# Pooled attention with a feed-forward behind it: the first weights' conversion put at other steps of a pair

## The chip, the cores and the metric

The kernel runs on one core of a Trainium2 chip. The metric is the device time of one execution in microseconds. A change is judged against the kernel before, timed on the same chip.

## The reference

Attention over 4 x 8 heads of 1152 keys and a head size of 64. Two neighbouring queries are averaged, so 576 are left; the scores are scaled, the row maximum is taken off, and the exponentials are normalised. The result, 2304 tokens of 512, goes through a feed-forward layer with 2048 hidden units:

```python
q_pool = q.reshape(B, H, S // 2, 2, D).mean(axis=3)
scores = scale * np.matmul(q_pool, k.transpose(0, 1, 3, 2))
attn = np.exp(scores - np.max(scores, axis=-1, keepdims=True))
attn = attn / (np.sum(attn, axis=-1, keepdims=True) + 1e-09)
x = np.matmul(attn, v)            # then heads side by side: (2304, 512)
r = np.maximum(x @ w_in, 0.0)
out = (s * (r * r) + b) @ w_out
```

The two weight matrices arrive as 64-bit floats. The kernel turns each into two 32-bit parts, hi and lo.

## The kernel before, in words

The kernel has two stages. The attention runs over 32 heads, two heads (a pair) at a time, 16 pairs from 0 to 15; the feed-forward layer follows.

A head has 9 steps, one for each block of 128 keys, so a pair has 18 steps, and a step number below is n % 18 of the loop over n. In a step TensorE makes the scores of one block (`score_step`, tile s, L486), ScalarE takes their exponentials (L490, L495, L498), and, where the step's kind in `KIND` asks for a high and a low part, VectorE (kind v) or GpSimd (kind g) makes pl, what the rounded exponential ph leaves over (L501). Kind w makes neither. The kinds of a pair are vwvgvwvgw, twice. GpSimd's pl belong to steps 3, 7, 12 and 16. Three steps later (`LAG`) TensorE multiplies the exponentials by v (`value_step`, tile o): L518 for kind w, else L524, L526 (with vl, the low part of v) and L528 (with pl). The order of TensorE's products in a step is written out in `ORD`.

Fifteen steps ahead, `max_unit` makes the scores again at lower cost (tile m, L456) and VectorE takes their row maximum (tile pm, L457) for the shift of a later head. Tile m has two PSUM banks, so a product waits until VectorE is through with the maximum two before it; tile s has two banks as well. At steps 2 and 11 `finish` copies the sums of a head out (ScalarE), and after the odd head VectorE inverts them (`XT`: transposes lt and rr, a reciprocal), and GpSimd scales (xo).

Other work of a pair stands at fixed steps: `PREP` prepares the pair after the next (transposes on VectorE at steps 10 to 12; on GpSimd qs at 9, kh at 11 and 12, kl at 12, qh and qz at 13, ql at 14); `prep_v` splits the next head's v at steps 7 and 16 (GpSimd, vv then vl); `load_k` and `load_q` follow at 14, `load_v` at 3 and 12, and `lay`, the copies of k and q into their tiles, at 4 and 13. All these DMAs are issued by SP, in that order; ScalarE issues the two small ones of the shift.

Engines work through their own queues in the order in which the program emits. What is put off goes through `later(k, fn)`, and `tick()` runs at the end of each step what is due. Put off by 0 or 1, an operation comes at the end of the same step; put off by k, ahead of the work of k steps on. Operations due at the same tick run by due time, then in the order in which they were put off.

The weights of the first three blocks of 128 hidden units are converted inside the attention (`conversions`, called with `wstage`, `STA` and no PSUM pool): six chunks of 128 x 512, w_in and w_out by turns. `CB` and `CP` say at which n a call comes: seven calls, 18 steps apart, the last at n = 274, step 4 of pair 15. A call at chunk i fetches chunk i + 1 (one DMA of 512 KB on SP) and starts `narrow(i)`, which has these parts, put off by the numbers of `STA`:

- s0 (L151, L153): ScalarE takes the absolute value of the high words into hm and scales the low words into R
- s1 (L159), s1b (L163), s1c (L166): VectorE clamps hm, shifts its bits and joins them with the sign into A
- s2 (L169, L170): VectorE keeps the exponent of A (ab), ScalarE rounds A to hi
- s3 (L174), s4 (L177), s5 (L180): GpSimd multiplies R by ab, subtracts hi from A, and adds both into lo

The tiles hm, ab, A and R exist once each, the raw chunk twice. Before the change s0 comes at the end of step 4, s1, s1b and s1c all ahead of step 8, s2 ahead of step 10, and s3, s4 and s5 ahead of steps 13, 15 and 17. Pairs 10 to 15 convert one chunk each; pair 9 has the first fetch alone. The other 26 chunks are converted in the feed-forward stage with other numbers (`STB`) and a PSUM tile.

```python
    def tick():
        step[0] += 1
        due = sorted(x for x in queue if x[0] <= step[0])
        queue[:] = [x for x in queue if x[0] > step[0]]
        for _, _, fn in due:
            fn()
...
            if (CB - n) % CP == 0 and 0 <= CB - n < 7 * CP:
                weights_a()
        tick()
```

Of the kernel before, what the change touches and what calls it, by code (L numbers as in the profile page):

```python
# [12 lines left out]
AF = mybir.ActivationFunctionType  # L13
# [27 lines left out]
VS = (7, 16)  # L41
XT = (1, 2, 3, 4, 8)
SW = (3, 9)
CB, CP = 274, 18
WB = (7, 11)
STA = (0, 4, 4, 4, 6, 9, 11, 13)
STB = (0, 1, 2, 3, 4, 5, 6, 8)
MO = (2, 3, 6)
XS = (1, 2)
# [3 lines left out]
def f32(ap):  # L53
    return ap.bitcast(F32)
# [3 lines left out]
def attention_moe_kernel(ctx: ExitStack, tc: tile.TileContext, q, k, v, w_in, w_out, s_in, b_in, out):  # L58
    nc = tc.nc
# [35 lines left out]
    def weight_tiles(pool, f0, f1):  # L95
        n = f1 - f0
        ih = pool.tile([P, NC, n * P], F32R, name=f"wih{f0}")
        il = pool.tile([P, NC, n * P], F32R, name=f"wil{f0}")
        oh = pool.tile([P, n, DM], F32R, name=f"woh{f0}")
        ol = pool.tile([P, n, DM], F32R, name=f"wol{f0}")  # L100
        for i in range(n):
            f = f0 + i
            wi_hi[f] = ih[:, :, i * P:(i + 1) * P]
            wi_lo[f] = il[:, :, i * P:(i + 1) * P]
            wo_hi[f] = oh[:, i, :]
            wo_lo[f] = ol[:, i, :]

    def conversions(pool, stage, f0, f1, bufs, stages, psum=None):

        weight_tiles(pool, f0, f1)
        chunks = []
        for f in range(f0, f1):
            chunks.append((w_in[:, f * P:(f + 1) * P].rearrange("(c p) f -> p c f", p=P), wi_hi[f], wi_lo[f], f"i{f}"))
            chunks.append((w_out[f * P:(f + 1) * P, :].rearrange("p (c f) -> p c f", c=NC),
                           wo_hi[f].rearrange("p (c f) -> p c f", c=NC), wo_lo[f].rearrange("p (c f) -> p c f", c=NC), f"o{f}"))
        wide = w_in.dtype == mybir.dt.int64
        raw = {}  # L120
        state = [-1]

        def done(i):
            f = f0 + i // 2
            ready[f] = ready.get(f, 0) + 1

        def tmp(tag, name):
            return stage.tile([P, NC, P], F32, tag=tag, bufs=bufs, name=f"{tag}{name}")

        def fetch(i):  # L130
            src, _, _, name = chunks[i]
            if wide:
                raw[i] = stage.tile([P, NC, 2 * P], I32, tag="wst", bufs=2, name=f"wst{name}")
                nc.sync.dma_start(raw[i], src.bitcast(I32))
            else:
                raw[i] = stage.tile([P, NC, P], F32, tag="wst", bufs=2, name=f"wst{name}")
                nc.sync.dma_start(raw[i], src)

        def narrow(i):
            _, hi, lo, name = chunks[i]  # L140
            words = raw.pop(i).rearrange("p c (n w) -> p c n w", w=2)
            high, low = words[:, :, :, 1].bitcast(F32), words[:, :, :, 0].bitcast(U32)
            hm, ab, A, R = (tmp(t, name) for t in ("whm", "wab", "wA", "wR")) if psum is None else (None, *(tmp(t, name) for t in ("wab", "wA", "wR")))

            bank = None if psum is None else psum.tile([P, 512], F32, tag="w", bufs=1, name=f"w{name}").rearrange("p (c f) -> p c f", c=NC)
            hm, bits, full = (hm, ab, A) if psum is None else (bank, bank, bank)
            hmi, biti, abi, fulli, top = (t.bitcast(I32) for t in (hm, bits, ab, full, high))
            eng = nc.gpsimd if psum is None else nc.vector

            def s0():  # L150
                nc.scalar.activation(hm, high, AF.Abs)  # L151
                if psum is None:
                    nc.scalar.activation(R, low, AF.Copy, scale=2.0 ** -52)  # L153
                else:
                    nc.gpsimd.tensor_scalar(out=R, in0=low, scalar1=2.0 ** -52, scalar2=0.0, op0=ALU.mult, op1=ALU.add)

            def s1():

                nc.vector.tensor_scalar(out=hm, in0=hm, scalar1=W_MIN, scalar2=W_MAX, op0=ALU.max, op1=ALU.min)  # L159

            def s1b():

                nc.vector.tensor_scalar(out=biti, in0=hmi, scalar1=0x07FFFFFF, scalar2=3, op0=ALU.bitwise_and, op1=ALU.logical_shift_left)  # L163

            def s1c():
                nc.vector.scalar_tensor_tensor(out=fulli, in0=top, scalar=-0x40000000, in1=biti, op0=ALU.bitwise_and, op1=ALU.bitwise_or)  # L166

            def s2():
                nc.vector.tensor_scalar(out=abi, in0=fulli, scalar1=-0x800000, scalar2=None, op0=ALU.bitwise_and)  # L169
                nc.scalar.activation(hi, full, AF.Copy)  # L170

            def s3():

                nc.gpsimd.tensor_tensor(out=R, in0=R, in1=ab, op=ALU.mult)  # L174

            def s4():
                eng.tensor_tensor(out=A, in0=full, in1=f32(hi), op=ALU.subtract)  # L177

            def s5():
                nc.gpsimd.tensor_tensor(out=lo, in0=A, in1=R, op=ALU.add)  # L180
                done(i)

            for at, fn in zip(stages, (s0, s1, s1b, s1c, s2, s3, s4, s5)):
                later(at, fn)

        def split(i):
            _, hi, lo, _ = chunks[i]
            st = raw.pop(i)
            nc.scalar.activation(hi, st, AF.Copy)

            def rest():
                nc.gpsimd.tensor_tensor(out=lo, in0=st, in1=f32(hi), op=ALU.subtract)
                done(i)

            later(stages[4], rest)

        def go():
            i = state[0]
            if i >= len(chunks):
                return False  # L200
            if i + 1 < len(chunks):
                fetch(i + 1)
            if i >= 0:
                (narrow if wide else split)(i)
            state[0] += 1
            return True

        return go
# [12 lines left out]
    def later(k, fn):  # L221
        step[1] += 1
        queue.append((step[0] + k, step[1], fn))
# [393 lines left out]
    lays = {}  # L617
    weights_a = conversions(wa, wstage, 0, SW[0], 1, STA)
    NS = NH * NJ
# [132 lines left out]
```

## Time and profile before

| what | us |
|---|---|
| three runs | 971.0, 973.78, 974.75; median 973.78 |
| the profiled execution, its own time | 976.95 |
| its span, first to last instruction | 975.2 |
| mean granted TensorE clock in it | 0.997 of full speed |
| busy: TensorE, VectorE, ScalarE, GpSimd | 922.3, 627.0, 545.9, 507.5 |

The profile is of one execution. Times in it count from the first instruction. Each engine has a timeline; an instruction's row gives its start, its duration, its line in the kernel, the tiles it writes and reads, their shapes, and in square brackets how long the engine stood idle before it and what ended that. The chain of waits follows the end of the program back to what released each step. The granted clock is what the chip allowed TensorE, as a share of 2.4 GHz. The attention's last score product starts at 553.2 us of the span, the first product of the feed-forward layer at 557.2.

### The profile page before, as it was taken

What the parts mean: (1) busy time and instruction counts of PE and PEld (TensorE: products, weight loads), DVE (VectorE), ACT (ScalarE), POOL (GpSimd) and SP (SyncE); (2) the same over time, 40 slices, a digit from 0 to 9 for tenths busy, and PEclk for the clock granted to TensorE, in tenths of its full rate; (3) what the DMA queues carried; (4) which work ended last, traced back from release to release, by engine and by line L of the source; (5) the groups of instructions that cost most, each with busy time, mean ns of one, the idle gap of its engine ahead of it and who ended that gap; (6) DMA issues with size and microseconds to landing.
All of it is one profiled execution on the core that took longest, in us unless ns stands there. A gap on an engine that the chain in (4) does not pass through costs nothing.

```text
span 975.2 us, 16173 instructions
## 1 busy us (share of the span) xinstructions
PE 922.3 (95%) x5712; PEld 821.4 (84%) x5712; DVE 627.0 (64%) x1168; ACT 545.9 (56%) x1054; POOL 507.5 (52%) x405
## 2 busy tenths in 40 slices
PE   4999999999999998988989989999999999999998
PEld 3888888888888887877877877889999899999997
DVE  5777776777677776876875376776776653334333
ACT  2766666666676675665767755554444443333332
POOL 6567656665667568568665567665353430110000
PEclk9999999999999999999999999999999999999999
DMA  8878776777767776676754155663544332222211
GB/s 149 167 145 169 158 152 122 154 168 147 134 138 167 156 152 147 153 142 138 165 146 102 35 162 164 205 217 130 174 130 158 104 136 78 66 87 90 84 44 44
DMA packets 255312, 131.17 MB, mean 135 GB/s; under 512 B 203776, under 2 KB 227328, under 8 KB 255232
## 3 DMA queue, kind: packets, MB, share of 16 engines
q1 hardware_dynamic: 244512, 129.62, 55.0%
q10 hardware_dynamic: 10720, 0.52, 0.7%
q8 instruction: 46, 0.75, 0.3%
q14 instruction: 34, 0.28, 0.1%
HBM read 68.68 MB, written 18.87 MB: 90 GB/s over the span
## 4 chain that ended last, share of the span: by engine, by line
PE 67%; ACT 12%; POOL 7%; DVE 5%; DMA 3%; issue 3%; ACTq 1%; SPq 0%; DVEq 0%; POOLq 0%
PE h L272 18%; PE y L299 17%; PE s L486 12%; PE o L518 5%; PE m L456 5%; PE o L524 4%; PE o L528 4%; PE o L526 4%; ACT ph L495 3%; ACT xu L544 2%; ACT l L545 2%; ACT s L498 2%; POOL pl L501 1%; DVE pm L457 1%; DMA wsto<-in_moe_w_out_dram 1%
## 5 line engine op out<-in xcount | busy, mean ns | idle before, releaser
L457 DVE TENSOR_REDUCE pm<-m 128x1 f32<-128x384 f32 x432 | 230.6, 549 | 112.8 <-PE m L456 106.9
L486 PE MATMUL s<-qq,kk 128*128 128x288 f32 x1152 | 217.6, 311 | 10.9 <-ACT pe L498 7.8
L272 PE MATMUL h<-x,wih 128*128 128x256 f32 x1152 | 213.3, 283 | 7.1 <-DVE gl L286 6.0
L272 PEld LDWEIGHTS h<-x,wih 128*128 128x128 f32 x1152 | 186.0, 189 | 22.1 <-DVE gl L286 6.4
L495 ACT ACTIVATE ph<-s 128x576 fp32r<-128x576 f32 x192 | 125.2, 652 | 132.4 <-PE s L486 109.8
L486 PEld LDWEIGHTS s<-qq,kk 128*128 128x128 f32 x1152 | 175.6, 191 | 27.2 <-ACT pe L498 11.0
L501 POOL TENSOR_TENSOR pl<-pe,ph 128x576 fp32r<-128x576 f32 x64 | 91.5, 1429 | 141.8 <-ACT pe L498 131.2
L272 PE MATMUL h<-x,wil 128*128 128x256 f32 x576 | 162.2, 282 | 0.0
L456 PE MATMUL m<-kh,qz 128*128 128x384 f32 x384 | 156.9, 418 | 3.2 <-DVE pm L457 3.1
L253 POOL TENSOR_TENSOR x<-xr,x 128x1024 fp32r<-128x1024 f32 x27 | 65.0, 2406 | 152.0 <-ACT x L212 143.1
L280 DVE SCALAR_TENSOR_TENSOR h<-h,sb,r 128x256 f32<-128x256 f32 x144 | 70.2, 487 | 114.5 <-ACT r L289 114.5
L524 PE MATMUL o<-ph,vv 128*128 128x288 f32 x384 | 119.0, 310 | 7.8 <-issue 4.8
L518 PE MATMUL o<-pe,vf 128*128 128x288 f32 x384 | 126.0, 412 | 0.0
L528 PE MATMUL o<-pl,vv 128*128 128x288 f32 x384 | 113.6, 296 | 7.3 <-POOL pl L501 7.3
L289 ACT ACTIVATE r<-h 128x256 f32<-128x256 f32 x144 | 55.6, 386 | 110.0 <-PE h L272 109.8
L501 DVE TENSOR_TENSOR pl<-s,ph 128x576 fp32r<-128x576 f32 x128 | 96.2, 752 | 30.9 <-ACT s L498 24.7
L526 PE MATMUL o<-ph,vl 128*64 128x288 f32 x384 | 113.6, 296 | 0.0
L299 PE MATMUL y<-wol,gh 128*128 128x512 f32 x288 | 113.1, 393 | 0.0
L299 PE MATMUL y<-woh,gl 128*128 128x512 f32 x288 | 112.9, 392 | 0.0
L299 PE MATMUL y<-woh,gh 128*128 128x512 f32 x288 | 112.6, 391 | 0.0
L272 PEld LDWEIGHTS h<-x,wil 128*128 128x128 f32 x576 | 109.6, 190 | 0.0
L283 ACT ACTIVATE gh<-h,sb 128x256 fp32r<-128x256 f32 x144 | 68.0, 473 | 64.6 <-DVE h L280 64.3
(89 smaller groups left out, 1508.6 us busy)
## 6 DMA issues: line engine op xcount, KB each, us to landing
kk<-kh SPq DMA_DIRECT2D x32, 576.0 KB, 6.0
kraw<-in_k_dram SPq DMA_DIRECT2D x64, 144.0 KB, 3.5
vf<-in_v_dram SPq DMA_DIRECT2D x32, 288.0 KB, 4.0
kk<-kT SPq DMA_DIRECT2D x32, 288.0 KB, 4.6
qq<-qh SPq DMA_DIRECT2D x64, 144.0 KB, 5.8
xr<-xd SPq DMA_DIRECT2D x18, 512.0 KB, 4.1
qraw<-in_q_dram SPq DMA_DIRECT2D x122, 72.0 KB, 2.5
wsti<-in_moe_w_in_dram SPq DMA_DIRECT2D x16, 512.0 KB, 4.9
```

Source lines behind the costliest of these rows:

```text
L272: nc.tensor.matmul(h[:, :TB], st[:, c, :], mv[:, c, :], start=(n == 0), stop=(n == 3 * NC - 1))
L280: nc.vector.scalar_tensor_tensor(out=t, in0=h[:, :TB], scalar=sb[:, 0:1], in1=r, op0=ALU.mult, op1=ALU.mult)
L299: nc.tensor.matmul(y[:, :DM], st[:, ts_], mv, start=(first and n == 0), stop=(last and n == 2))
L456: nc.tensor.matmul(ps[:, :KB], st, khs[p][:, e * KB:(e + 1) * KB], start=True, stop=True)
L457: nc.vector.tensor_reduce(out=pms[p][:, col, e:e + 1], in_=ps[:, :KB], axis=AX.X, op=ALU.max)
L486: nc.tensor.matmul(ps[:, a, :HALF], kk[:, i, j * P:(j + 1) * P], qq[:, i, a], start=(i == 0), stop=(i == 1))
L495: nc.scalar.activation(ph, ps[:, :, :HALF], AF.Exp, scale=SCALE)
L501: fresh.append(lambda: eng.tensor_tensor(out=pl, in0=full, in1=f32(ph), op=ALU.subtract))
L518: nc.tensor.matmul(o[:, :HALF], vfs[hd % 2][:, j], ph[:, a], start=first, stop=last)
L524: nc.tensor.matmul(o[:, :HALF], vv[:, j], ph[:, a], start=first, stop=False)
L526: nc.tensor.matmul(o[0:D, :HALF], vl[:, j], ph[:, a], start=False, stop=False)
L528: nc.tensor.matmul(o[:, :HALF], vv[:, j], pl[:, a], start=False, stop=last)
```

## The change

The calls come four steps earlier, at step 0 of a pair (`CB` 270 instead of 274), so the fetch of the next chunk does too. `STA` has new numbers: s0 at the end of step 0 with s1 right behind it, s1b ahead of step 3, s1c ahead of step 5, s2 ahead of step 7, and s3, s4, s5 ahead of steps 0, 1 and 2 of the next pair. R, the scaled low words, is made in s2 instead of s0 for these chunks. (Its one tile is still read by s5 of the chunk before until step 2.) The feed-forward stage's conversions stay as they are.

```diff
-CB, CP = 274, 18
+CB, CP = 270, 18
 WB = (7, 11)
-STA = (0, 4, 4, 4, 6, 9, 11, 13)
+STA = (0, 1, 3, 5, 7, 18, 19, 20)
...
             def s0():
                 nc.scalar.activation(hm, high, AF.Abs)
-                if psum is None:
-                    nc.scalar.activation(R, low, AF.Copy, scale=2.0 ** -52)
-                else:
+                if psum is not None:
                     nc.gpsimd.tensor_scalar(out=R, in0=low, scalar1=2.0 ** -52, scalar2=0.0, op0=ALU.mult, op1=ALU.add)
...
             def s2():
                 nc.vector.tensor_scalar(out=abi, in0=fulli, scalar1=-0x800000, scalar2=None, op0=ALU.bitwise_and)
                 nc.scalar.activation(hi, full, AF.Copy)
+                if psum is None:
+                    nc.scalar.activation(R, low, AF.Copy, scale=2.0 ** -52)
```

## Rows read from the trace of the kernel before

Rows of a timeline: start us, duration us, engine, line, operation, tiles, shapes, count, [idle us before it <- what ended it].

**Rows 1.** The page's chain that ended last, share of the span by engine

```profile
PE 67%; ACT 12%; POOL 7%; DVE 5%; DMA 3%; issue 3%; ACTq 1%; SPq 0%; DVEq 0%; POOLq 0%
```

**Rows 2.** TensorE's timeline: first score product of pairs 9, 10 and 14 (start, us)

```profile
315.23 0.91 PE L486 MATMUL s<-qq,kk 128*128 128x288 f32 x4
...
347.26 0.91 PE L486 MATMUL s<-qq,kk 128*128 128x288 f32 x4
...
489.06 0.91 PE L486 MATMUL s<-qq,kk 128*128 128x288 f32 x4
```

**Rows 3.** Waits by line: us in total, times, longest

```profile
PE o L528 <- POOL pl L501: 7.3, 4, 2.1
```

**Rows 4.** GpSimd's timeline at the start of pair 11

```profile
382.80 1.29 POOL L177 TENSOR_TENSOR wAi<-wAi,wih 128x512 f32<-128x512 f32 x1
...
384.05 1.39 POOL L501 TENSOR_TENSOR pl<-pe,ph 128x576 fp32r<-128x576 f32 x1
```

**Rows 5.** TensorE's timeline: waits in pair 11 (two) and pair 14

```profile
385.50 0.40 PE L528 MATMUL o<-pl,vv 128*128 128x288 f32 x1 [1.83 <-POOL pl L501]
...
401.46 0.44 PE L456 MATMUL m<-kh,qz 128*128 128x384 f32 x1 [0.59 <-DVE pm L457]
...
508.81 0.44 PE L456 MATMUL m<-kh,qz 128*128 128x384 f32 x1 [0.60 <-DVE pm L457]
```

**Rows 6.** Stretch behind the first of them: busy time by engine, granted clock, DMA

```profile
386.00:389.50 3.50, 3.50 (x14) 2.91 (x13) 0.56 (x1) 2.26 (x6) 2.69 (x3) 0.55 0.18 30
```

**Rows 7.** VectorE's timeline: conversion's operations in pairs 10 (one) and 11 (two)

```profile
363.76 0.69 DVE L166 SCALAR_TENSOR_TENSOR wAi<-wsti,wabi 128x512 int32<-128x512 int32 x1
...
398.24 0.41 DVE L159 TENSOR_SCALAR whmo<-whmo 128x512 f32<-128x512 f32 x1
...
399.20 1.73 DVE L166 SCALAR_TENSOR_TENSOR wAo<-wsto,wabo 128x512 int32<-128x512 int32 x1
```

**Rows 8.** GpSimd's timeline in pair 9

```profile
316.32 1.43 POOL L501 TENSOR_TENSOR pl<-pe,ph 128x576 fp32r<-128x576 f32 x1
...
318.47 1.43 POOL L431 TENSOR_TENSOR vl<-vf,vv 128x576 fp32r<-128x576 f32 x1
...
323.92 1.42 POOL L501 TENSOR_TENSOR pl<-pe,ph 128x576 fp32r<-128x576 f32 x1 [4.02 <-ACT pe L498]
...
331.67 0.67 POOL L214 TENSOR_SCALAR vv<-vf 128x576 fp32r<-128x576 f32 x1 [0.36 <-DMA vf<-in_v_dram]
```

**Rows 9.** VectorE's timeline in pair 9

```profile
320.01 1.21 DVE L457 TENSOR_REDUCE pm<-m 128x1 f32<-128x384 f32 x2 [1.26 <-PE m L456]
...
321.34 0.75 DVE L501 TENSOR_TENSOR pl<-s,ph 128x576 fp32r<-128x576 f32 x1
...
324.18 1.21 DVE L457 TENSOR_REDUCE pm<-m 128x1 f32<-128x384 f32 x2 [0.52 <-PE m L456]
...
325.31 0.75 DVE L501 TENSOR_TENSOR pl<-s,ph 128x576 fp32r<-128x576 f32 x1
...
326.66 1.73 DVE L457 TENSOR_REDUCE pm<-m 128x1 f32<-128x384 f32 x3
...
330.79 1.21 DVE L457 TENSOR_REDUCE pm<-m 128x1 f32<-128x384 f32 x2 [1.27 <-PE m L456]
```

**Rows 10.** TensorE's timeline in pair 9

```profile
327.46 0.34 PE L456 MATMUL m<-kh,qz 128*128 128x384 f32 x1
...
337.54 0.29 PE L526 MATMUL o<-ph,vl 128*64 128x288 f32 x1
```

**Rows 11.** Groups by line and form (busy us, mean ns, idle before)

```profile
L174 POOL TENSOR_TENSOR wRi<-wRi,wabi 128x512 f32<-128x512 f32 x16 | 20.7, 1294 | 22.1 <-DVE wabi L169 18.5 <-DMA yq<-yd_True 3.7
...
L153 ACT ACTIVATE wRi<-wsti 128x512 f32<-128x512 uint32 x3 | 2.0, 658 | 0.0
```

**Rows 12.** ScalarE's timeline in pair 9

```profile
328.63 0.65 ACT L495 ACTIVATE ph<-s 128x576 fp32r<-128x576 f32 x1 [0.42 <-PE s L486]
```

**Rows 13.** The page's DMA issues (times, KB each, us to landing)

```profile
wsti<-in_moe_w_in_dram SPq DMA_DIRECT2D x16, 512.0 KB, 4.9
```

## The prediction

> **What bounds the kernel now.** I read the chain of waits first: TensorE carries 67% of the span, ScalarE 12%, GpSimd 7% and VectorE 5% [rows 1]. So TensorE sets the time, and another engine counts only where it makes TensorE wait. The change touches only the six weight chunks converted inside the attention (pairs 10 to 15), so the next view is TensorE's timeline at the first score product of a pair. Pair 9, which only fetches a chunk, runs from 315.23 to 347.26, that is 32.03 us. Pairs 10 to 13, which convert one chunk each, run from 347.26 to 489.06, that is 141.80 us or 35.45 each [rows 2]. Four pairs like pair 9 would take 128.12. The conversions, which should lie beside TensorE's work, therefore cost 141.80 - 128.12 = 13.7 us there.
>
> Two waits make up most of that. The waits by line show TensorE's L528 (the product with pl) waiting for GpSimd's pl of L501, 7.3 us in 4 waits [rows 3]. The timelines show why. At the start of pair 11 GpSimd does the conversion's s4 (wAi) and only then, at 384.05, the pl of step 16 [rows 4], and TensorE stands idle 1.83 us, until 385.50, for that pl [rows 5]. In pair 9 the same pl starts at 316.32, 1.1 us after the pair's first score product [rows 2, 8], and nothing waits. The difference is s3 and s4, queued ahead of it. The second wait is VectorE's: three operations in a row ahead of step 8 (the first 0.41 us, the last 1.73) push the next row maximum back, and TensorE waits 0.59 us for that maximum's PSUM bank at 401.46 and 0.60 us at 508.81 [rows 5, 7]. A third loss follows the first: in the 3.5 us after the wait of pair 11 the granted clock is 0.55 on average [rows 6], mostly the lower level, 1.2 GHz; it fell behind those 1.83 us of standing idle.
>
> **The change part by part.** The sum is made against the profiled execution, 976.95 us. That is 3.17 above the median of the three runs, 973.78, so I work out the difference and take it from the median.
>
> Removed: the 13.7 us of pairs 10 to 13, and in pair 14 the fourth of the waits for pl and the wait at 508.81. Of the four waits' 7.3 us I take a quarter, 1.8, plus 0.6: 2.4. Pair 15 computes no row maxima, and I count nothing there. Together 16.1 us, if nothing new takes their place.
>
> s3, s4, s5 (GpSimd, 1.29 us each by L174; the other two have the same shape [rows 11]) move behind pl, vv and vl of step 16 and ahead of the pl of step 3. In pair 9 GpSimd ends vl at 319.90 and is idle 4.02 us until that pl at 323.92 [rows 8]. Three operations need 3.87 us, or 3.75 at the 1.25 us from one start to the next (382.80 to 384.05 [rows 4]). They fit with 0.15 to 0.27 us to spare. Behind them is queued the pl of step 3. Its product stands three steps later, and a pair's mean step is 32.03 / 18 = 1.78 us, so some 5.3 us from the score of that step against two exponentials (0.65 us each [rows 12]) and 1.43 us of subtraction [rows 8]. A lateness of half a microsecond is covered; beyond about 2 us TensorE would wait again. Cost taken: 0.
>
> s1 (VectorE, 0.41 us clean [rows 7]) now stands right behind step 0's subtraction, in the same tick as the Abs that it needs. That subtraction lasts about as long as Abs, so VectorE hardly waits, and ahead of the row maxima of step 2 it idles 1.26 us [rows 9]. Cost 0, between 0 and 0.5 if it is blocked for 1.73.
>
> s1b (same form, 0.41) comes behind step 2's subtraction, from about 322.1 [rows 9]. GpSimd is then in s4 or s5, so it may be blocked until that operation ends: 0.4 to 1.73 us. There are 0.52 us of idle time ahead of the maxima at 324.18 [rows 9]. I take the end of s4 as it would fall in pair 9 (319.90 + 2 x 1.25 = 322.4), about 0.7 us in all, so 0.2 is left over for VectorE's queue and nothing for TensorE. Cost 0, bounds 0 and 1.2.
>
> s1c (0.69 clean at 363.76, 1.73 blocked [rows 7]) follows step 4's subtraction at 326.0. From 324.18 to 330.79 VectorE has no gap [rows 9], so the three maxima of 326.66 start 0.69 later and the first of the three, a third of 1.73, ends at 327.9. TensorE's m product at 327.46 [rows 10] writes the bank which that maximum empties. It waits about 0.5 us. The pl of step 3, at 323.92, is over by then (325.34 [rows 8]), so I take the clean duration. Cost 0.5 in each of pairs 10 to 14, bounds 0 and 1.7.
>
> s2 (again that form, 0.41) ahead of step 7 meets the 1.27 us of idle time ahead of 330.79 [rows 9]: cost 0, bounds 0 and 1.2. On ScalarE the copy to hi and R (0.66 each [rows 11]) now precede step 7's exponentials, which had 0.42 us of idle time in front of them [rows 12]. They come 0.9 us late, and the pl made from them 0.9 us late, with the same three steps in hand: cost 0. R leaves step 4, where it stood ahead of step 5's exponential; I count no gain for it.
>
> The fetch (512 KB, one DMA on SP's queue) is now ahead of load_v at step 3 and the lay at step 4, which it followed. GpSimd's vv waits 0.36 us for that load in pair 9 and starts at 331.67; with its 0.67 us and a vl of 1.43 behind it, vl is ready at 333.8 [rows 8], and TensorE first uses it at 337.54 [rows 10], so 3.7 us are in hand. A fetch takes 4.9 us from issue to landing [rows 13]; if the load waited for all of it, TensorE would wait 1.2 us. Bounds 0 and 1.2, in five pairs 0 to 6. I take 0, since transfers share the engines and the fetch is issued before the load.
>
> Sum: 16.1 - 5 x 0.5 = 13.6 us. 976.95 - 13.6 = 963.35 for the profiled execution, 973.78 - 13.6 = 960.2 for the median.
>
> **The rivals.** A measurement of this kernel can tell about 0.5%, 4.9 us, from no change: faster begins below 968.9, slower above 978.6.
>
> *The wait moves.* GpSimd's room of 4.02 us is filled to 0.15. If VectorE's s1 or s1b holds GpSimd up, or vl of step 16 comes later in a pair with a conversion, pl of step 3 is late and its product waits as step 16's did. Price: as much as now, 7.3 us, so 967.5. For it: the tight fit. Against it: the product's three steps.
>
> *The load of v is late behind the fetch.* 1.2 us in each of five pairs is 6.0: 966.2. For it: vv already waits for this load. Against it: 3.7 us in hand.
>
> *VectorE's operations collide one by one, and the kernel gets slower.* An operation that starts while GpSimd works lasted 1.73 us where its clean price is 0.69 [rows 7]. Today one burst meets one GpSimd operation; tomorrow four operations stand at four places. If s1b, s1c and s2 are all blocked, the stretch from 322 to 331 takes 1.73 x 3 = 5.2 us more against idle times of 0.52 and 1.27: 3.4 us a pair. Waits of that length bring the lower clock as in pair 11, 3.5 us at 0.55, some 1.6 us more. (3.4 + 1.6) x 5 = 25.0, so 973.78 - 16.1 + 25.0 = 982.7. It decides from (16.1 + 4.9) / 5 = 4.2 us a pair. Against it: s1c, the longest of them, stands behind the end of pl in pair 9.
>
> The Trainium skill (SBUF — State Buffer, section Who interferes with whom) has the rule behind this rival: VectorE in a two-port mode or with two SBUF inputs, and GpSimd, hold one shared port pair as an exclusive lock for a whole instruction, and the one issued second blocks fully, so that splitting a burst does not make its parts safe. The 1.73 us agrees. By the rule alone, with the lock held each time, the time would be this rival's 982.7; by the rows, where s1c meets no GpSimd operation and the other two have idle time behind them, it is 960.2.
>
> *It is not the conversion.* If the preparation alone made pl late, nothing would go. Pair 9 has the same preparation without the wait, so this gets little.
>
> **How the numbers follow.** Forecast 0.70; the wait moves 0.12; the load of v 0.08; collisions 0.04; no change, or half of the gain eaten by several of the upper bounds, 0.06. The forecast's own range goes from 956.5 (nothing new, 973.78 - 16.1 = 957.7, and 1.2 for pair 15 and the runs' scatter) to 965. For 8 in 10 I reach to the two middle rivals: 956.0 to 968.5. Faster: 0.70 + 0.08 + most of 0.12 = 0.87. Same 0.09. Slower 0.04.
>
> **What would show it.** Right: L528 no longer waits for GpSimd's pl at step 1 of pairs 11 to 14; the clock stays at 1.0 through the attention; pairs 10 to 13 last about 32.5 us; a wait of half a microsecond for a row maximum at step 5 instead of step 8; s3 to s5 back to back behind vl. Wrong: L528 waiting at step 6, VectorE's operations at 1.5 us and more, vv late, or pairs still over 34 us.

## The result and the profile after

| | before | changed |
|---|---|---|
| median (lowest to highest), us | 974.26 (971.0 to 975.57), 4 runs | 961.41 (959.34 to 962.38), 4 runs |
| ratio of the times, 95% interval | | 0.9868 (0.9849 to 0.9887) |
| the profiled execution, its own time | 976.95 | 962.38 |
| its span | 975.2 | 960.4 |
| first product of the feed-forward layer | 557.2 | 541.9 |

The changed kernel is faster by 12.9 us, and by its interval by 11.0 to 14.7. In the two profiled executions the span falls by 14.8 us: the attention ends 15.3 us earlier, the feed-forward layer takes 418.5 us where it took 418.0.

The page of the changed kernel, busy time of each engine and the chain that ended last (share of the span by engine), the second line against [rows 1]:

```profile
PE 915.8 (95%) x5712; PEld 818.2 (85%) x5712; DVE 621.5 (65%) x1168; ACT 546.4 (57%) x1054; POOL 507.0 (53%) x405
...
PE 72%; ACT 13%; DVE 4%; DMA 3%; issue 2%; POOL 2%; ACTq 1%; SPq 0%; POOLq 0%; DVEq 0%
```

TensorE is busy for 915.8 us against 922.3 with as many instructions, and VectorE for 621.5 against 627.0. ScalarE and GpSimd are as before. What changed is the chain: GpSimd falls from 7% to 2% of it.

TensorE's timeline of the changed kernel, first score products of pairs 9, 10, 11 and 14, against [rows 2]:

```profile
314.24 0.91 PE L486 MATMUL s<-qq,kk 128*128 128x288 f32 x4
...
346.58 0.91 PE L486 MATMUL s<-qq,kk 128*128 128x288 f32 x4
...
379.05 0.91 PE L486 MATMUL s<-qq,kk 128*128 128x288 f32 x4
...
476.35 0.91 PE L486 MATMUL s<-qq,kk 128*128 128x288 f32 x4
```

Pairs 10 to 13 now take 476.35 - 346.58 = 129.77 us where they took 141.80: 12.0 less. The same kind of row gives the length of every pair, from 9 to 15 (the last one to its last step):

```
pair            9      10     11     12     13     14     15
before          32.03  33.39  36.60  34.92  36.89  36.25  27.93
changed         32.34  32.47  32.42  32.39  32.49  33.92  27.70
```

Pair 14 gives another 2.3 us. About 1 us of the 15.3 lies ahead of pair 9 (314.24 against 315.23), where no chunk is converted; I count it as scatter between two executions.

GpSimd's timeline of the changed kernel at the start of pair 11, against [rows 4] and, for the preparation without a conversion, [rows 8]:

```profile
380.24 1.44 POOL L501 TENSOR_TENSOR pl<-pe,ph 128x576 fp32r<-128x576 f32 x1
381.64 0.69 POOL L214 TENSOR_SCALAR vv<-vf 128x576 fp32r<-128x576 f32 x1
382.41 1.47 POOL L431 TENSOR_TENSOR vl<-vf,vv 128x576 fp32r<-128x576 f32 x1
383.84 1.28 POOL L174 TENSOR_TENSOR wRi<-wRi,wabi 128x512 f32<-128x512 f32 x1
385.08 1.27 POOL L177 TENSOR_TENSOR wAi<-wAi,wih 128x512 f32<-128x512 f32 x1
386.44 1.35 POOL L180 TENSOR_TENSOR wil<-wAi,wRi 128x512 fp32r<-128x512 f32 x1
387.74 1.43 POOL L501 TENSOR_TENSOR pl<-pe,ph 128x576 fp32r<-128x576 f32 x1
```

This is the picture to look for: pl of step 16 comes first, 1.19 us behind the pair's first score product, vv and vl follow, then s3, s4 and s5 back to back, and pl of step 3 right behind them, without idle time in any row. That pl starts 387.74 - 379.05 = 8.69 us into the pair, and in pair 9 of before it was 323.92 - 315.23 = 8.69 as well. Three operations entered the queue and pl is not a tenth of a microsecond late.

VectorE's timeline of the changed kernel in the same pair, with s1 (L157), s1b (L161), s1c (L164) and s2 (L167) one by one:

```profile
382.01 0.60 DVE L157 TENSOR_SCALAR whmo<-whmo 128x512 f32<-128x512 f32 x1
...
385.82 0.82 DVE L161 TENSOR_SCALAR wabo<-whmo 128x512 int32<-128x512 int32 x1
...
389.80 0.68 DVE L164 SCALAR_TENSOR_TENSOR wAo<-wsto,wabo 128x512 int32<-128x512 int32 x1
...
391.09 1.61 DVE L457 TENSOR_REDUCE pm<-m 128x1 f32<-128x384 f32 x3
...
393.29 0.42 DVE L167 TENSOR_SCALAR wabo<-wAo 128x512 int32<-128x512 int32 x1
```

TensorE's timeline there:

```profile
391.67 0.45 PE L456 MATMUL m<-kh,qz 128*128 128x384 f32 x1 [0.23 <-DVE pm L457]
```

s1c runs at its clean price and pushes the three maxima back, and the m product behind the first of them waits. In this pair step 6 takes 2.27 us where pair 9 of before takes 1.78: half a microsecond. The product's own row shows 0.23 of it as a wait; the weight load ahead of it stood idle for 0.47.

Waits by line in the changed kernel (us in total, times, longest); against [rows 3] there is no line in which L528 waits:

```profile
POOL vv L214 <- DMA vf<-in_v_dram: 11.5, 7, 3.2
...
PE m L456 <- DVE pm L457: 1.4, 5, 0.5
```

The stretch of the conversions, busy time by engine (PE, PEld, DVE, ACT, POOL), then the granted clock, DMA share and GB/s:

```profile
340.00:542.00 202.00, 193.06 (x1210) 172.08 (x1208) 144.85 (x262) 144.70 (x266) 138.40 (x111) 1.00 0.66 142
```

The clock is 1.00 throughout, where [rows 6] had 0.55 behind the wait of pair 11.

### The profile page after: what moved, and what is told of

It reads as the page before. It is cut to its first block, busy times and chain, and to the rows that moved or that the text cites. A ratio compares the mean times of both kernels' runs of the same rounds, so it can differ in the third digit from the quotient of the medians.

```text
span 960.4 us, 16166 instructions
## 1 busy us (share of the span) xinstructions
PE 915.8 (95%) x5712; PEld 818.2 (85%) x5712; DVE 621.5 (65%) x1168; ACT 546.4 (57%) x1054; POOL 507.0 (53%) x405
## 4 chain that ended last, share of the span: by engine, by line
PE 72%; ACT 13%; DVE 4%; DMA 3%; issue 2%; POOL 2%; ACTq 1%; SPq 0%; POOLq 0%; DVEq 0%
PE h L272 18%; PE y L299 17%; PE s L486 14%; PE o L518 6%; PE m L456 5%; PE o L524 4%; PE o L526 4%; PE o L528 4%; ACT ph L495 4%; ACT xu L544 2%; ACT s L498 2%; ACT l L545 2%; DMA xr<-xd 2%; DVE pm L457 1%; ACT pe L498 1%
## 5 line engine op out<-in xcount | busy, mean ns | idle before, releaser
L486 PEld LDWEIGHTS s<-qq,kk 128*128 128x128 f32 x1152 | 173.5, 190 | 26.2 <-ACT pe L498 9.0
L518 PE MATMUL o<-pe,vf 128*128 128x288 f32 x384 | 123.2, 405 | 0.0
L501 DVE TENSOR_TENSOR pl<-s,ph 128x576 fp32r<-128x576 f32 x128 | 96.4, 753 | 37.6 <-ACT s L498 32.6
L528 PE MATMUL o<-pl,vv 128*128 128x288 f32 x384 | 112.8, 294 | 0.0
```

Of the source, the lines that this page charges most:

```text
L486: nc.tensor.matmul(ps[:, a, :HALF], kk[:, i, j * P:(j + 1) * P], qq[:, i, a], start=(i == 0), stop=(i == 1))
L501: fresh.append(lambda: eng.tensor_tensor(out=pl, in0=full, in1=f32(ph), op=ALU.subtract))
L518: nc.tensor.matmul(o[:, :HALF], vfs[hd % 2][:, j], ph[:, a], start=first, stop=last)
L528: nc.tensor.matmul(o[:, :HALF], vv[:, j], pl[:, a], start=False, stop=last)
```

## The experiments

All but the first start from the changed kernel, and the diffs are against it. In each I read the length of pairs 10 to 14 in TensorE's timeline, because the feed-forward stage itself varies by some 3 us between executions (415.7 in the first experiment, 418.5 in the changed kernel): the medians alone don't settle a microsecond. The time of the first feed-forward product stands beside them, but it carries scatter from ahead of the conversions as well: pair 9 starts anywhere from 313.4 to 315.9 us. Each row of pairs is one execution. Each ratio is to the kernel before, timed on the same chip.

```
                  median  ratio to before (95%)    10    11    12    13    14    sum   first ff product
before            974.26                         33.39 36.60 34.92 36.89 36.25 178.05  557.2
changed           961.41  0.9868 (.9849-.9887)   32.47 32.42 32.39 32.49 33.92 163.69  541.9
GpSimd's part     963.34  0.9867 (.9839-.9895)   33.19 33.47 33.32 33.33 34.46 167.77  545.5
VectorE's part    974.41  0.9980 (.9962-.9999)   32.66 36.06 35.95 35.30 36.15 176.12  554.3
burst at 5        966.61  0.9902 (.9868-.9937)   34.34 34.44 33.43 33.67 35.11 170.99  548.9
s5 three times    973.46  0.9969 (.9952-.9987)   32.61 34.33 35.81 34.48 35.57 172.80  552.7
s1b at 1          974.03  1.0000 (.9985-1.0015)  32.66 36.92 33.56 35.74 36.59 175.47  555.9
s1b at 1, s2 at 8 975.37  1.0015 (1.0001-1.003)  32.60 35.58 35.55 34.96 37.25 175.94  554.6
s1c at 7          960.83  0.9873 (.9854-.9892)   32.71 32.03 32.73 32.42 33.07 162.96  542.3
two tiles ab      963.84  0.9911 (.9884-.9938)   32.47 32.45 32.18 32.57 36.00 165.67  543.9
changed again     961.05  0.9877 (.9858-.9895)   32.55 33.00 32.58 32.96 34.05 165.14  542.9
```

### GpSimd's operations moved alone

In the kernel before, s3, s4 and s5 are put at steps 0, 1 and 2 of the next pair, and nothing else:

```diff
-STA = (0, 4, 4, 4, 6, 9, 11, 13)
+STA = (0, 4, 4, 4, 6, 14, 15, 16)
```

> The kernel before, with s3, s4 and s5 alone moved, ahead of steps 0, 1 and 2 of the next pair; VectorE's three operations stay one behind the other ahead of step 8. Theory: GpSimd's queue ahead of the pl of step 16 was the larger part. TensorE's four waits for that pl and the two falls of the clock behind them go, which is some 2.0 us in each of pairs 11 to 14 and 0.9 more in two of them, about 10 us in all: 964 us. The burst stays: pairs 10 to 13 at 33.2 to 33.4 us, with a wait of 0.6 us for a row maximum in step 9. Rival: the burst was the larger part, then 969 or more.

The median is 963.34 us (962.93 to 963.84), ratio 0.9867 (0.9839 to 0.9895). The line of L528 among the waits is gone, and TensorE's waits for a row maximum are what is left:

```profile
PE m L456 <- DVE pm L457: 4.2, 6, 0.8
```

The clock is 1.00 from 340 us on. The pairs stand at 33.2 to 33.5 us, a microsecond over the changed kernel's, and step 9, behind the burst, at 2.4 to 2.5. Over pairs 10 to 14 this part alone brings 178.05 - 167.77 = 10.3 us of the change's 14.4. This is the larger term of the sum, and the theory holds for it. The medians can't tell it from the whole change (0.9867 and 0.9868); the pairs can.

### VectorE's operations moved alone

s0 to s2 stay as changed; s3, s4 and s5 go back to their old steps. The earlier fetch and the new place of R stay too, so they are in this part and were not tried by themselves:

```diff
-STA = (0, 1, 3, 5, 7, 18, 19, 20)
+STA = (0, 1, 3, 5, 7, 13, 15, 17)
```

> The changed kernel, with s3, s4 and s5 ahead of steps 13, 15 and 17, as before the change. Theory: the waits for the pl of step 16 come back in pairs 11 to 14, 1.7 to 2.1 us each, some with the lower clock behind them; the burst's loss stays away and the wait of step 6 is there. 961.4 + 8.4 + 0 to 3.5 = 970 to 973 us, pairs 11 to 13 at 34.4 us or more. Rival, that taking VectorE's burst apart brought most of it: 965 or less, no wait for pl.

Median 974.41 us (972.47 to 975.93), ratio 0.998 (0.9962 to 0.9999), 1.4 us above the expected range; pairs 10 to 14 are 178.05 - 176.12 = 1.9 us shorter. The waits by line have L528 back, and longer than before:

```profile
PE o L528 <- POOL pl L501: 9.0, 4, 2.4
```

GpSimd's timeline at the start of pair 11 shows part of why it grew from 7.3 to 9.0. VectorE's s1 stands at step 0 now and runs beside the late pl, which takes 1.58 us instead of the 1.39 of [rows 4]; it also starts 3.60 us into the pair instead of 3.40:

```profile
381.56 1.28 POOL L177 TENSOR_TENSOR wAi<-wAi,wih 128x512 f32<-128x512 f32 x1
382.80 1.58 POOL L501 TENSOR_TENSOR pl<-pe,ph 128x576 fp32r<-128x576 f32 x1
```

And the lower clock follows the waits, as in [rows 6], in two places (columns as in the stretch above):

```profile
384.00:388.00 4.00, 3.57 (x14) 3.21 (x14) 0.09 (x1) 1.87 (x4) 3.62 (x4) 0.57 0.39 62
422.00:425.50 3.50, 3.50 (x12) 2.93 (x12) 1.45 (x4) 2.81 (x6) 1.77 (x2) 0.55 0.01 1
```

Together the two parts bring 10.3 + 1.9 = 12.2 us of the 14.4. They don't quite add. VectorE's part alone lost 1.7 us in longer waits for the late pl; with GpSimd's part in place, where no such wait is left, it is worth 167.77 - 163.69 = 4.1 us. The second execution of the changed kernel (the last row of the table) puts that at 2.6, so the size of the interplay is known to a microsecond or two only.

### The burst kept whole, at a place where it isn't blocked

s1 and s1b are put off by 5 like s1c. The three stand in a row again, but ahead of step 5, where GpSimd has nothing to do:

```diff
-STA = (0, 1, 3, 5, 7, 18, 19, 20)
+STA = (0, 5, 5, 5, 7, 18, 19, 20)
```

> The changed kernel, with s1, s1b and s1c put together again, all ahead of step 5, where GpSimd is idle in pair 9; GpSimd's operations stay where the change put them. Theory: a maximum waits for all that stands ahead of it on VectorE, blocked by GpSimd or not. The three take 0.41 + 0.43 + 0.69 = 1.5 us instead of 0.7 for s1c alone, so the wait for the maximum's bank in step 6 grows from 0.2 to 1.0 us idle and each of pairs 10 to 14 by 0.8: 965.5 us, pairs at 33.2. Rival, that the burst only cost because GpSimd blocked its last operation: no more than now, 961.4, pairs at 32.4.

Median 966.61 us (965.96 to 967.66), ratio 0.9902 (0.9868 to 0.9937). VectorE's timeline in pair 11:

```profile
391.24 0.42 DVE L157 TENSOR_SCALAR whmo<-whmo 128x512 f32<-128x512 f32 x1
...
391.76 0.43 DVE L161 TENSOR_SCALAR wabo<-whmo 128x512 int32<-128x512 int32 x1
...
392.28 0.69 DVE L164 SCALAR_TENSOR_TENSOR wAo<-wsto,wabo 128x512 int32<-128x512 int32 x1
...
393.58 1.61 DVE L457 TENSOR_REDUCE pm<-m 128x1 f32<-128x384 f32 x3
```

TensorE's timeline, its wait behind them:

```profile
394.16 0.45 PE L456 MATMUL m<-kh,qz 128*128 128x384 f32 x1 [1.28 <-DVE pm L457]
```

All three are clean, 1.54 us in sum, and yet TensorE waits 1.28 us for the maximum, where s1c alone makes it wait 0.23. Step 6 takes 3.31 us instead of 2.27. So at this step a burst costs by its bare length in front of the maxima, about 1 us a pair, and a burst in a quiet place is still a burst. The rival, that a clean burst would do as well here, falls. Of the burst's old place, ahead of step 8, this says less: there one of its operations ran about 1.04 us over its clean price and TensorE waited 0.59, so a clean burst may have cost nothing there. That wasn't tried.

Two of the pairs hold something else. In pair 11 step 14 takes 3.42 us instead of 2.53; ScalarE's issue of L472 took 1.69 us there, and the last experiment takes that up. Pair 10 is long because in pair 9 the load of v, which now follows the fetch, came late, as GpSimd's timeline shows:

```profile
335.15 0.67 POOL L214 TENSOR_SCALAR vv<-vf 128x576 fp32r<-128x576 f32 x1 [5.01 <-DMA vf<-in_v_dram]
```

GpSimd's queue then ran without a gap from there to the pl of step 16, and TensorE's timeline in pair 10 has the price:

```profile
349.95 0.40 PE L528 MATMUL o<-pl,vv 128*128 128x288 f32 x1 [0.85 <-POOL pl L501]
```

### The cover of the pl of step 3 measured

s5 runs three times, which holds GpSimd for two more operations ahead of the pl of step 3:

```diff
-                nc.gpsimd.tensor_tensor(out=lo, in0=A, in1=R, op=ALU.add)
+                for _ in range(3 if psum is None else 1):
+                    nc.gpsimd.tensor_tensor(out=lo, in0=A, in1=R, op=ALU.add)
```

> The changed kernel, with s5 done three times in a row for the attention's chunks (it writes the same lo each time). This puts 2.6 us more of GpSimd's time ahead of the pl of step 3. Theory of the prediction: some 2 us of lateness are covered by the three steps until the product. The pl then comes 2.5 us late and TensorE waits 0.5 to 1 us in step 6 of pairs 11 to 14: 963.5 to 966 us. Rival, that the three operations fit into the gap with nothing in hand behind it: each tenth of lateness is paid, 2.5 us in four or five pairs, 971 us or more.

Median 973.46 us (969.34 to 974.63), ratio 0.9969 (0.9952 to 0.9987). The attention is 552.7 - 541.9 = 10.8 us longer than the changed kernel's, far more than expected. The time is the one that the rival gave, so the rows have to say whether the cause is the rival's too. Lines behind the edit are one higher here. GpSimd's timeline in pair 11:

```profile
380.05 1.43 POOL L502 TENSOR_TENSOR pl<-pe,ph 128x576 fp32r<-128x576 f32 x1
...
386.25 4.09 POOL L181 TENSOR_TENSOR wil<-wAi,wRi 128x512 fp32r<-128x512 f32 x3
390.29 1.42 POOL L502 TENSOR_TENSOR pl<-pe,ph 128x576 fp32r<-128x576 f32 x1
```

TensorE's timeline, the two waits:

```profile
391.77 0.40 PE L529 MATMUL o<-pl,vv 128*128 128x288 f32 x1 [0.60 <-POOL pl L502]
...
393.44 0.44 PE L457 MATMUL m<-kh,qz 128*128 128x384 f32 x1 [1.15 <-DVE pm L458]
```

VectorE's timeline, what stands behind the second of them:

```profile
390.37 1.89 DVE L164 SCALAR_TENSOR_TENSOR wAo<-wsto,wabo 128x512 int32<-128x512 int32 x1 [0.51 <-POOL wil L181]
```

The first wait is what I was after. The pl of step 3 starts 390.29 - 379.04 = 11.25 us into the pair, where the changed kernel has 8.69, so it is 2.56 us late. Its product starts 12.73 us into the pair. TensorE's timeline of the changed kernel has the same product at 391.01 - 379.05 = 11.96:

```profile
391.01 0.29 PE L528 MATMUL o<-pl,vv 128*128 128x288 f32 x1
```

So 2.56 us of lateness cost 0.77, and the cover is 1.8 us. The changed kernel says the same directly: its pl ends at 389.17, 1.84 us ahead of that product. The rival, that every tenth is paid, falls for this pl. The second wait was overlooked. s1c of the new chunk writes tile A, which s5 of the chunk before still reads, and A exists once. VectorE stands idle 0.51 us for that, and then runs 1.89 us beside the pl instead of 0.69; the row maxima behind it come late, and TensorE waits 1.15 us. In the changed kernel s5 ends at 387.79 and s1c starts at 389.80, so 2.0 us are in hand there. With both waits step 6 takes 4.05 to 4.26 us in pairs 11 to 14, where the changed kernel takes 2.25 to 2.51. Behind those of pair 12 the clock falls as well (0.59 on average from 428.5 to 432), and in pair 15 the product waits 1.87 us for its pl.

### s1c behind the three maxima, first try

Since s1c costs half a microsecond a pair, I moved it to step 7, behind the three maxima, and s2 to step 10; to keep room I also put s1b at step 1:

```diff
-STA = (0, 1, 3, 5, 7, 18, 19, 20)
+STA = (0, 1, 1, 7, 10, 18, 19, 20)
```

> The changed kernel, with s1b behind s1 ahead of step 1, s1c ahead of step 7 and s2 ahead of step 10. Theory: the only loss that is left is s1c in the gapless stretch of VectorE ahead of step 6's maxima. Ahead of step 1 there are 1.26 us idle against 0.41 + 0.43, ahead of step 8 there are 1.27 against 0.69. The wait of step 6 goes, 0.5 us in each of pairs 10 to 14: 959 us, pairs 10 to 13 at 31.9 to 32.0. Rival, that s2 ahead of step 10 meets GpSimd's split of v, which now comes later: up to 1.5 us of VectorE's time ahead of step 11, then as much as is gained is lost and the pairs stay at 32.4 or more.

And the same with s2 at step 8, to see whether s2 beside a pl costs anything:

```diff
-STA = (0, 1, 3, 5, 7, 18, 19, 20)
+STA = (0, 1, 1, 7, 8, 18, 19, 20)
```

> As the run with s2 ahead of step 10, but with s2 ahead of step 8, where GpSimd does the pl of step 7. Theory: the wait of step 6 goes as well; s2 is blocked until that pl ends and delays the maxima of step 8 by some 0.8 us, of which TensorE sees 0.2 to 0.3: pairs 10 to 13 at 32.2, 960 us. Rival, that a blocked operation there costs nothing: 32.0, 959 us; or that ScalarE's two conversions ahead of step 8 hold back its exponentials: 33 and more.

Medians 974.03 us (971.14 to 977.77), ratio 1.0 (0.9985 to 1.0015), and 975.37 (973.4 to 978.33), ratio 1.0015 (1.0001 to 1.003). Neither the theories nor the rivals named what happened: the whole gain is lost. The wait in step 6 is gone, as meant, but VectorE's timeline of the first of the two shows a worse one:

```profile
386.49 1.47 DVE L161 TENSOR_SCALAR wabo<-whmo 128x512 int32<-128x512 int32 x1 [2.54 <-POOL wRi L174]
```

TensorE's timeline has the price:

```profile
388.49 0.69 PE L456 MATMUL m<-kh,qz 128*128 128x384 f32 x1 [2.69 <-DVE pm L457]
```

s1b writes tile ab, which s3 of the chunk before still reads (wRi is its output), and ab exists once. VectorE stood still 2.54 us for it, with two row maxima queued behind. Then it was blocked beside wAi on top of that, 1.47 us instead of 0.42. The second kernel has the same wait, 2.52 us. Its s2, beside a pl, lasts 1.56 us and makes step 9 take 1.81 us where it takes 1.50: 0.3 us, as the theory said, but under a loss some ten times as large.

### s1c at 7 with s1b left at 3, and s1b at 1 with two tiles ab

If the tile ab is the cause, either of two edits mends it: leave s1b where the change has it, or give ab two buffers.

```diff
-STA = (0, 1, 3, 5, 7, 18, 19, 20)
+STA = (0, 1, 3, 7, 10, 18, 19, 20)
```

> The changed kernel, with s1c ahead of step 7 and s2 ahead of step 10; s1b stays ahead of step 3, after the time at which GpSimd has done s3 of the chunk before. Theory: the run with s1b ahead of step 1 lost its time to the one tile ab, since s1b writes what s3 still reads, and not to s1c or s2. Here that wait is not there and the wait of step 6 goes: pairs 10 to 13 at 32.0 to 32.2, 959 to 960 us, 1 to 2 below the changed kernel. Rival, that s1c or s2 at their new places caused the loss: pairs at 35 and 974 us, as there.

```diff
-STA = (0, 1, 3, 5, 7, 18, 19, 20)
+STA = (0, 1, 1, 7, 10, 18, 19, 20)
...
-            return stage.tile([P, NC, P], F32, tag=tag, bufs=bufs, name=f"{tag}{name}")
+            return stage.tile([P, NC, P], F32, tag=tag, bufs=2 if tag == "wab" else bufs, name=f"{tag}{name}")
```

> The run with s1b ahead of step 1 again (s1c ahead of step 7, s2 ahead of step 10), with one thing more: the tile ab twice. Theory: VectorE then waits for nothing of GpSimd's in step 1, it is only blocked until vl ends, as in pair 10 of that run, which has no chunk before it (1.5 us, pair 32.66). Pairs 11 to 13 come to 32.2 to 32.8: 961 us. Rival, that GpSimd's operations one behind the other keep VectorE out until the last is done, whatever the tiles: 974 us, as there.

With s1b at step 3 the median is 960.83 us (959.93 to 962.65), ratio 0.9873 (0.9854 to 0.9892). With two tiles it is 963.84 (962.18 to 968.57), ratio 0.9911 (0.9884 to 0.9938), and VectorE's timeline has s1b without the wait:

```profile
381.37 1.52 DVE L161 TENSOR_SCALAR wabo<-whmo 128x512 int32<-128x512 int32 x1
```

GpSimd's timeline has the vl beside which it ran, and the wRi behind:

```profile
381.14 1.47 POOL L431 TENSOR_TENSOR vl<-vf,vv 128x576 fp32r<-128x576 f32 x1
382.57 1.45 POOL L174 TENSOR_TENSOR wRi<-wRi,wabi 128x512 f32<-128x512 f32 x1
```

Pairs 10 to 13 are back at 32.2 to 32.6 us. So the single tile was the cause in the two kernels above, and a blocked s1b by itself (1.52 us here) costs nothing there: steps 2 and 3 take 2.43 + 1.74 = 4.17 us, as they do in pair 9 of before (1.85 + 2.32). Pairs 14 and 15 are longer (36.0 and 28.9 us). In pair 14 TensorE's long waits are for ScalarE's exponentials, 0.73 us at step 4 and 1.65 at step 16; what brings the second I didn't follow.

Neither beats the change. With s1c at 7 and s1b at 3, step 6 takes 1.78 us again and pair 11 comes to 32.03 us, the length of a pair without a conversion; but pairs 10 and 12 lose 0.6 to 0.7 us in steps 11 to 14, and pair 13 loses 0.35 in step 4. There s1b ran blocked for 1.51 us beside s5, and TensorE's weight load for the m product stood idle 0.53 us for a row maximum: at step 3 a fully blocked s1b does cost something. In the changed kernel steps 12 to 14 of pair 11 take about 0.2 us less in sum than in pair 9 of before (2.61 + 1.45 + 2.53 against 3.31 + 1.57 + 1.89); with s1c at 7 step 12 of pair 11 is as long as it was. A wait that the changed kernel itself has there can be read in TensorE's timeline of the changed kernel, at step 14 of pair 11:

```profile
406.77 0.77 PE L486 MATMUL s<-qq,kk 128*128 128x288 f32 x4 [0.47 <-DVE pl L501]
```

ScalarE's timeline has what stands behind that pl, the issue of the second small DMA of the shift (L472, on ScalarE's queue) and the exponential that follows it:

```profile
403.80 0.79 ACTq L472 DMA_DIRECT2D qq<-c  x1
404.64 0.65 ACT L495 ACTIVATE ph<-s 128x576 fp32r<-128x576 f32 x1 [1.18 <-PE m L456]
```

The exponential starts 0.05 us behind the end of the issue. Why a wait at step 12 comes and goes with the place of s1c was not tried.

### The changed kernel once more

The same kernel beside the last two, on the same chip:

> The changed kernel once more, on the same chip as these two, to stand beside them: 960 to 962.5 us, pairs 10 to 13 at 32.4 to 32.5.

Median 961.05 us (959.72 to 963.57), ratio 0.9877 (0.9858 to 0.9895), pairs 10 to 13 at 32.6 to 33.0. Expected were 32.4 to 32.5. So a pair's length carries some half a microsecond from one execution to the next, and 960.83 with s1c at 7 is no better. The scatter of these pairs has one source. Pair by pair, this is the time that ScalarE spent on the issue of L472 in pairs 10 to 13, and the pair's length less that time:

```
                 issue of L472           pair less issue
changed          0.84 0.79 0.77 0.85     31.63 31.63 31.62 31.64
changed again    0.93 1.38 0.97 1.34     31.62 31.62 31.61 31.62
```

All else in these eight pairs agrees within 0.03 us. In pairs 9 to 13 of the kernel before the same issue takes 0.56 or 0.57; what makes it longer here is not shown.

## Why the prediction was right

Forecast 960.2, measured 961.41; the difference to before was forecast as 13.6 and measured as 12.9 by the medians and 14.6 by the two profiled executions' own times. The mechanism came out as the trace of before had it, and its places with the exceptions named below. By steps:

- **The removed waits, 13.7 and 2.4.** Right. L528 no longer waits, the clock stays at 1.00, and pairs 10 to 13 are within 0.5 us of a pair without conversion. The subtraction of four pairs like pair 9 was the number that counted: it took waits, slow clock and burst in one, without having to price the clock. The single runs of the two parts split the 14.4 us of pairs 10 to 14 as 10.3 (GpSimd) and 1.9 (VectorE), the rest coming only with both in place.
- **s1c, 0.5 in each of five pairs.** Right in mechanism; step 6 takes 2.25 to 2.27 us in pairs 10 to 13 against 1.78. That the whole pairs agree as well is partly luck: they exceed 4 x 32.03 by 129.77 - 128.12 = 1.65 us, 0.4 each, because steps 12 to 14 came out shorter; in the second execution of the changed kernel, with longer issues of L472, the excess is 0.7 each. In the traces the wait stands in step 6 by the score product ahead of it, one step behind where I wrote it (as the old one stands in step 9, not 8). The row of 330.79 was misread there: VectorE's stretch without a gap ends 1.27 us ahead of it, at 329.52. The term doesn't change by that.
- **s3 to s5 at nothing.** Right: from the start of s3 to that of pl it is 387.74 - 383.84 = 3.90 us (forecast 3.87 or 3.75), and pl of step 3 starts at the same 8.69 us of the pair. "Beyond about 2 us TensorE would wait again" was measured: 1.8 us.
- **s1 and s1b at nothing.** Right: 0.60 and 0.82 us in pair 11, the 0.82 near the 0.7 forecast, and no TensorE wait follows. In that second execution s1 ran blocked for 1.48 and 1.56 us in pairs 12 and 14, and pair 12 is no longer for it. For s1b the bounds were needed: with s1c at 7 a blocked one cost 0.35 us in pair 13. But the working had one condition too few. That s1b may start at step 3 at all rests on s3 of the chunk before being through with the tile ab; s3 ends at 385.12 and s1b starts at 385.82, 0.7 us in hand. The same holds for s1c, s5 and tile A, with 2.0 us. I named the tiles for R alone. It cost nothing here, and two steps earlier it cost the whole gain.
- **s2 and ScalarE's copies at nothing.** Right: s2 is clean (0.42), and hi and R at step 7 show up in no wait of TensorE's.
- **The load of v behind the fetch, 0 (bounds 0 and 1.2).** Right for the changed kernel. GpSimd's vv does wait longer for it, 11.5 us in 7 waits with 3.2 the longest, against 6.4 in 6 with 2.5 the longest before; the longest is still inside the 3.7 us in hand, and no wait of TensorE's comes of it. But the working looked only at the product with vl. GpSimd's queue carries the lateness on to the pl of step 16, and where the load came 5.0 us late (burst at 5, pair 9) TensorE waited 0.85 us for that.
- **Pair 14.** Counted as 2.4 less 0.5, it gave 2.3. It remains the longest, 33.92 us; its step 14 took 3.54 us before and takes 3.67 now, behind an issue of L472 that lasts 2.49 us before and 2.65 now. The change didn't touch that operation.

Of the rivals, *the wait moves* needed the pl of step 3 late by more than its cover, and in pairs 11 to 13 it is late by 0.05 us at most. *The load of v* was late and covered. *The collisions* are what the experiments speak to most. Blocked operations of VectorE did appear, at 1.47 to 1.89 us, and one of 2.32 in the changed kernel itself (s1b in pair 15, which computes no row maxima). Where idle time stood behind them (s1b in the kernel with two tiles) they cost nothing; beside a pl s2 cost 0.3 us, and s1b at step 3 cost 0.35. The rule of the Trainium skill (SBUF — State Buffer, section Who interferes with whom), that VectorE and GpSimd hold the shared port pair as an exclusive lock and the second one is blocked, agrees with these rows. But the rival's price of 3.4 us a pair, worked out from the 1.73 us of [rows 7], needed three blocked operations in every pair, and no run shows that. A blocked operation cost more where something was late already: s1 beside the late pl, where it went with a longer wait for that pl, s1b behind its wait for the tile ab, and s1c with s5 three times, where it stood ahead of the maxima. *It is not the conversion* falls with the first experiment.

## What to carry to other kernels

When an in-order engine feeds the bound engine, put the deadline-free work right behind the operation that is waited for, not ahead of it, and size the gap from a stretch of the trace that does the same work without the extra: the difference between the two stretches is the whole prize, slow clock included. Split a burst on an engine that serves short deadlines even where nothing blocks it, if the engine has no idle time ahead of them. Before moving an operation earlier, list for each tile that exists once who still reads it: here 0.7 us lay between a gain of 13 us and none.

## What the runs showed of the hardware

A VectorE operation that was blocked by GpSimd did not wait for GpSimd's queue to drain: s1b, 385.82 to 386.64 in the changed kernel, ends 0.29 us behind wAi (386.35), and the next GpSimd operation, wil, which starts at 386.44, takes 1.35 us instead of the 1.28 to 1.29 that it takes in the first and the third experiment. GpSimd pays for it too: wRi takes 1.45 us behind the blocked s1b of the kernel with two tiles, 1.28 in the changed kernel.

The granted clock doesn't fall behind every wait, and not by their length alone. With VectorE's part alone TensorE waited 4 times for pl. Behind the waits of 2.21 and 2.31 us (pairs 11 and 12) the clock was at the lower level for a while (0.57 and 0.55 in the stretches above); behind those of 2.40 and 2.11 (pairs 13 and 14) it stayed at 1.00. So a wait of about 2 us has two prices, with or without the slow microseconds behind it: pairs 11 and 12 took 36.06 and 35.95 us, pair 13 took 35.30.

On ScalarE, what is queued behind a DMA issue starts only when the issue has ended. In every pair from 9 to 14 of both executions of the changed kernel the next exponential starts 0.04 or 0.05 us behind the end of L472's issue, and that issue takes from 0.60 to 2.70 us. The longest two, 2.65 and 2.70 in pair 14, stand beside an issue on SP's queue (L406) of 2.70 and 2.59.
